# One pair of heads per TensorE round, one slot for V and two for K, in a cached decode block

## The chip, the cores and the metric

The kernel runs on one core of a Trainium2 chip. The metric is the device time of one execution in microseconds (us). The kernel before takes 1302.85 us, the median of three runs (1302.77 to 1302.91).

## The reference

The block decodes one token for two sequences. It has an attention part over a long cache and a small MLP, both with a layernorm ahead of them.

```python
def _A_ref(x, k_cache, v_cache, wq, wo):          # x: 2 x 1 x 512
    B, Sq, D = x.shape
    H, Dh = 32, 128                                # caches: 2 x 32 x 8192 x 128, f32
    q = (x @ wq).reshape(B, Sq, H, Dh).transpose(0, 2, 1, 3)
    scores = einsum("bhqd,bhkd->bhqk", q, k_cache) * (Dh ** -0.5)
    p = softmax(scores, axis=-1)
    o = einsum("bhqk,bhkd->bhqd", p, v_cache)
    return o.transpose(0, 2, 1, 3).reshape(B, Sq, H * Dh) @ wo

def _B_ref(x, w1, b1, w2, b2):
    y = layernorm(x)
    h = gelu(einsum("bsd,df->bsf", y, w1) + b1)    # F = 1792
    return einsum("bsf,fd->bsd", h, w2) + b2

h = x + _A_ref(layernorm(x), ...)
h2 = h + _B_ref(layernorm(h), ...)
```

Each cache holds 268 MB of float32, and each element of it is used once. The profile counts 561 MB of reads in all.

## The kernel before

**Units.** The work is cut into 32 units, `units[i] = (g, b)`: a pair of heads g (16 pairs) of one sequence b (2). The units 2g and 2g+1 belong to one pair; they are called the even and the odd unit of pair g below. The K of a unit is a tile of 128 partitions x 16384 f32 (8.39 MB; partitions 0 to 63 hold one head, 64 to 127 the other), and so is its V. I write K(i) and V(i) for them.

**What a unit does.** VectorE (DVE) multiplies K(i) by the broadcast query (`multiply`, L468), in two pieces of 80 and 48 rows in most units (`LONG`), and sums each row (`add_up`, L476); GpSimd (POOL) first adds the halves of the 80-row piece (`halve`, L472), so that DVE has half as much to sum there. `row_max` (L483) takes each partition's maximum and TensorE (PE) transposes it. After the odd unit, `all_max` (L488) takes the maxima of both units, `exps` makes the exponentials of both on ScalarE (ACT, L503), and `values` multiplies them on PE with V: 32 products (64 in the records, since a float32 product takes two passes) that fill four groups of 32 output partitions in turn. `values(2g)` stands right behind `exps(g)`; `values(2g+1)` stands in the next unit, behind its second `multiply`. `gather` copies the result to SBUF, `head_sum` adds its four parts on PE, and `head_out` (L543) scales with the softmax's denominator.

**Slots and the order of loads.** SBUF has room for three tiles of K or V: the three slots of `kv`, handed out in turn by `slot()`. Unit i asks for V(i-1) and then K(i+1), and one queue (SP) issues all of these loads in that order. A load can't be issued before the last reader of its slot is done, and SP takes its entries strictly in turn, so a load that waits holds up all behind it. Going round three slots, V(n) comes into the slot of K(n), and K(n+3) into the slot of V(n). `Waits` sets all semaphore waits from what each instruction reads and writes; a DMA counts on one of 12 semaphores (`LANES`), in turn.

**TensorE's loop.** `Rounds` records PE's instructions of units between `pe.round()` calls, and `end` (L200) requires each round to have the same addresses and to move its waits by the same steps; then it writes one round as a loop body. Before, a round holds `GH = 3` pairs, and there are five rounds; the PSUM and SBUF buffers come round to the same place after three pairs. 72 tiny products on zeros (`SPARE`), whose result nobody reads, stand ahead of the loop.

**The attention output on its way to `wo`.** `head_out` writes rows: 4 partitions (sequence x head), three pairs wide (`orow`). Every three pairs `turn` transposes them on PE and `turned` adds them to columns (`oall`). `stage` brings the queries of three pairs at a time to the partitions where `make_q` spreads them. Part of `wo` (`wog`) is fetched by an indirect DMA onto chosen partitions.

**The end.** In the last unit (31) `load_wo` fetches `wo` and V(30) follows; then come V(31) and the MLP's weights. `project_all` multiplies the heads with `wo`, and the MLP follows.

Of the kernel before, what the change touches and what calls it, by code (L numbers as in the profile page):

```python
# [12 lines left out]
P = 128  # L13
# [7 lines left out]
SPARE = 72  # L21
GP = 6
GH = 3
SR = 4
LW = 6
LEFT = (((3, 7), (9, 16), (20, 28), (44, 47), (54, 57), (67, 93), (101, 106), (110, 114), (118, 122)),)
# [12 lines left out]
class Waits:  # L39
    LANES = 12  # L40

    def __init__(self, nc):
        self.nc = nc
        self.sems, self.count, self.clock, self.after, self.mem, self.mask = ({} for _ in range(6))
        self.lane = {}
        self.off = False
        nc.push_inst_callback(self.seen)
# [63 lines left out]
    def skip(self, n):  # L111
        self.lane["hard"] += n
# [5 lines left out]
    def place(self, eng, op, areas):  # L118
        areas = [(x, w) for x, w in areas if x is not None]
        queue = (eng,)  # L120
        if "DMA" in op:
            kind = "soft" if eng == "Pool" else "hard"
            k = self.lane.get(kind, 0)
            self.lane[kind] = k + 1
            proc = (kind, k % self.LANES)
        else:
            proc = queue
# [33 lines left out]
    def close(self):  # L161
# [3 lines left out]
        last = ("hard", (self.lane["hard"] - 1) % self.LANES)  # L165
# [80 lines left out]
class Room:  # L246
# [3 lines left out]
    def tile(self, shape, dtype, name, tag=None, bufs=None, ahead=0):  # L250
# [6 lines left out]
        ring.append(ring.pop(ahead))  # L257
        v = ring[-1][:shape[0], :n]
# [6 lines left out]

    def turn(self, key, n):
        ring = self.held[key]
        ring[:] = ring[n:] + ring[:n]


def tile_decode_block(nc, waits, x, k, v, wq, wo, wog, w1, bias, w2, out):
# [10 lines left out]
    GL = NP - 1  # L282
    units = [(g, b) for g in range(NP) for b in range(B)]
# [11 lines left out]
    def slot():  # L295
        return kv.tile([P, ROW], F32, name="kv", tag="kv")
# [7 lines left out]
    wqt = slot()  # L304
# [3 lines left out]
    wgt = wts.tile([P, len(LEFT), SR, D], F32, name="wgt")  # L308
# [8 lines left out]
    orow = const.tile([4, GH, 2, DH], F32, name="orow")  # L317
    oall = const.tile([P, 2, 2 * GP, B], F32, name="oall")
    NQ = len(LEFT)
    og = const.tile([P, NQ * SR + LW - TH, B], F32, name="og")  # L320
    slots = [kept(x) for x in LEFT]
    first_slot = [sum(n for _, n in slots[:q]) for q in range(len(LEFT))]
    HG = H - LW
    NS = (HG - 4 * GP) * DH // SR
    assert sum(n for _, n in slots) == NS
# [3 lines left out]
    pms = {}  # L329
    for x in LEFT:  # L330
        if x not in pms:
            pms[x] = const.tile([P, P], F32, name=f"pm{len(pms)}")
            nc.gpsimd.memset(pms[x], 0.0)
            for p0, s0, n in kept(x)[0]:
                nc.gpsimd.tensor_copy(pms[x][:, p0:p0 + n], ident[:, s0:s0 + n])
    pm = [pms[x] for x in LEFT]
    FAR = 4096.0
    ioff = const.tile([P, len(LEFT)], F32, name="ioff")
    for q in range(len(LEFT)):
        nc.gpsimd.tensor_scalar(ioff[:, q:q + 1], pidx, first_slot[q] - FAR, None, op0=ALU.add)  # L340
# [9 lines left out]
    so2 = [psa.tile([P, 512], F32, name="so"), [psq.tile([P, 512], F32, name="qps") for _ in range(3)][2]]  # L350
# [5 lines left out]
    qs = const.tile([2 * B, GH, DH], F32, name="qs")  # L356
    wz = const.tile([P, B], BF16, name="wz")
    nc.gpsimd.memset(wz, 0.0)
# [9 lines left out]
    y2 = wgt[:B, 0, 0, :]  # L368
    nc.vector.tensor_scalar(y2, x2, mv[:, 0:1], rs, op0=ALU.subtract, op1=ALU.mult)

    ypt = psm.tile([P, DC, B], F32, name="sm")
# [4 lines left out]
    ipt = psm.tile([P, len(LEFT)], F32, name="sm")  # L376
    for q in range(len(LEFT)):
        pe.matmul(ipt[:, q:q + 1], pm[q], ioff[:, q:q + 1], start=True, stop=True)
# [8 lines left out]
    i4 = ident[:4, :4].rearrange("m (b s) -> m b s", s=2)  # L387
    hmask = const.tile([4, 2], F32, name="hmask")
    nc.vector.tensor_add(hmask, i4[:, 0, :], i4[:, 1, :])

    gidx = const.tile([P, len(LEFT)], mybir.dt.int32, name="gidx")
# [13 lines left out]
    QP, S, MX, MT, GM, LT, RL, SS, OP, OT, TP = ({} for _ in range(11))  # L405
# [5 lines left out]
    def stage(m):  # L411
        g = GH * min(m, NP // GH - 1) + 1
        n = next((n for n in range(1, GH) if (g + n) % NG == 0), 1)
        for at, n in ((0, n), (n, GH - n)):
            rows, cols = of_pair(g + at)
            src = q2[rows, cols.start:cols.start + n * DH]
            nc.vector.tensor_reduce(qs[:, at:at + n].rearrange("m k d -> m (k d)"), src[:, :, None], axis=AX.X, op=ALU.max)  # L417

    def make_q(g):
        QP[g] = psq.tile([P, B, DH], F32, name="qps")  # L420
        for b in range(B):
            rows, cols = of_pair(g)
            q = qs[:, (g - 1) % GH, :] if g else q2[rows, cols]
            pe.matmul(QP[g][:, b], pick[:2 * B, b, :], q, start=True, stop=True)

    make_q(0)
    stage(0)
    rowacc = psa.tile([B, D], F32, name="rowacc")
    for _ in range(SPARE):
        pe.matmul(rowacc[:, :B], wz, wz, start=True, stop=True)  # L430

    def load(src, i, parts):
        g, b = units[i]
        t = slot()
        rows = src[b, 2 * g:2 * g + 2].rearrange("h (p j) d -> (h p) (j d)", j=NS2)
        for s0, n in parts:
            nc.sync.dma_start(t[:, s0 * DH:(s0 + n) * DH], rows[:, s0 * DH:(s0 + n) * DH])
        return t

    def load_wo():  # L440
        t = slot()
        n = (2 * 2 * GP + LW) * D
        t = t[:, ROW - n:]
        nc.sync.dma_start(t, wo)
        for q in range(NQ):
            nc.gpsimd.indirect_dma_start(
                out=wgt[:, q].rearrange("p r n -> p (r n)"), out_offset=None,
                in_=wog,
                in_offset=bass.IndirectOffsetOnAxis(ap=gidx[:, q:q + 1], axis=0),
                bounds_check=NS - 1, oob_is_err=False)  # L450
        tv = t[:, :2 * 2 * GP * D].rearrange("p (j r n) -> p j r n", j=2, n=D)
        return tv, t[:, 2 * 2 * GP * D:].rearrange("p (r n) -> p r n", n=D)

# [24 lines left out]
    def row_max(i):  # L478
        g, b = units[i]
        if not b:  # L480
            MX[g] = work.tile([P, B], F32, name="mx", bufs=3)
            MT[g] = psm.tile([1, B, P], F32, name="sm")
# [3 lines left out]
    def all_max(g):  # L486
        gm = work.tile([1, B, 2], F32, name="gm", bufs=3)
        nc.vector.tensor_reduce(gm, MT.pop(g).rearrange("o b (s p) -> o b s p", s=2), axis=AX.X, op=ALU.max,  # L488
                                negate=True)
        GM[g] = psm.tile([P, B, 2], F32, name="sm")  # L490
# [15 lines left out]
    def total(g):  # L506
        RL[g] = psm.tile([4, 1] if g < GL else [P, 4], F32, name="sm")
        if g < GL:
            pe.matmul(RL[g], lt4, ones[:, 0:1], start=True, stop=True)
        else:  # L510
            pe.matmul(RL[g], ones, lt4, start=True, stop=True)

    def inverse(g):
        r = work.tile(list(RL[g].shape), F32, name="rl" if g < GL else "rlp")
# [17 lines left out]
    def head_sum(g):  # L532
        ss = SS.pop(g)
        OP[g] = psm.tile([4, DH] if g < GL else [P, 2 * B], F32, name="sm")
        for j in range(4):
            sj = ss[:, j * DH:(j + 1) * DH]
            a, w = (sel4[:, :, j], sj) if g < GL else (sj, sel4[:, :, j])
            pe.matmul(OP[g], a, w, start=(j == 0), stop=(j == 3))

    def head_out(g):  # L540
        op, rl = OP.pop(g), RL.pop(g)
        if g < GL:
            nc.vector.scalar_tensor_tensor(orow[:, g % GH], op[:, None, :].to_broadcast([4, 2, DH]), rl,  # L543
                                           hmask[:, :, None].to_broadcast([4, 2, DH]), op0=ALU.mult, op1=ALU.mult)
# [4 lines left out]
    def turn(j):  # L549
        rows = orow.rearrange("m k e d -> m (k e d)")  # L550
        if j < 4:
            TP[j] = psm.tile([HP, 2 * GP, 2 * B], F32, name="sm")
            rows = rows.rearrange("m (p r) -> m r p", r=2 * GP)
            for r in range(2 * GP):
                pe.transpose(TP[j][:, r, :], rows[:, r, :], ident[:4, :4])
            psm.turn("sm", 2)
            return
        TP[j] = psm.tile([P, NQ * SR + LW - TH, 2 * B], F32, name="sm")
        at, n = (HG - 4 * GP) * DH, LW - TH
        last = rows[:, at:at + n * DH].rearrange("m (p r) -> m r p", r=n)  # L560
        for r in range(n):
            pe.transpose(TP[j][:, NQ * SR + r, :], last[:, r, :], ident[:4, :4])
        rows = rows.rearrange("m (s r) -> m r s", r=SR)
        for q, (_, n) in enumerate(slots):
            s0 = first_slot[q]
            for r in range(SR):
                pe.transpose(TP[j][:n, q * SR + r, :], rows[:, r, s0:s0 + n], ident[:4, :4])

    def turned(j):
        if j < 4:  # L570
            tp = TP.pop(j)
            half = slice(HP * (j % 2), HP * (j % 2 + 1))
            nc.vector.tensor_reduce(oall[half, j // 2], tp.rearrange("p r (b s) -> p r b s", b=B), axis=AX.X, op=ALU.add)
            return
# [271 lines left out]
```

## Time and profile before

| what | value |
|---|---|
| median of three runs | 1302.85 us (1302.77 to 1302.91) |
| profiled execution, span from first to last instruction | 1301.3 us |
| mean granted TensorE clock | 0.638 |
| DMA | 561.17 MB, mean 431 GB/s |
| busy: DVE / PE / POOL / ACT | 976.5 / 384.8 / 366.5 / 49.3 us |

No own device time of the profiled execution is listed beside its span; the median of the runs lies 1.55 us above the span. A row of the timeline has the start and the duration in us, the engine, the line, the operation and its operands, and in brackets how long the engine had been idle and what ended that. A row of the chain of waits has start, duration and what was going on. "SPq" is SP's queue: the rows are the moments at which it issues a load.

### The profile page before, as it was taken

How to read it: one execution, taken by the hardware profiler on the slowest of the kernel's cores; microseconds unless marked ns; L12 is line 12 of the kernel's file. 1: busy time of each engine (PE TensorE's matmuls, PEld its weight loads, DVE VectorE, ACT ScalarE, POOL GpSimd, SP SyncE). 2: the span in 40 equal slices, each digit the busy share in tenths (PEclk: the TensorE clock that was granted, in tenths of full speed). 3: DMA queues.
4: the chain of work that ended last, by engine and by line, in shares of the span. 5: the costliest groups of instructions: out<-in, count | busy, mean ns of one | idle time of the engine just before them, and what ended most of it. 6: DMA issues, size and time to landing. Idle time of an engine off the chain costs nothing.

```text
span 1301.3 us, 6543 instructions
## 1 busy us (share of the span) xinstructions
PE 384.8 (30%) x2890; PEld 118.5 (9%) x2890; DVE 976.5 (75%) x291; ACT 49.3 (4%) x157; POOL 366.5 (28%) x67
## 2 busy tenths in 40 slices
PE   3105023230412314033330513323032331502359
PEld 0001000000100001010000101001010100100113
DVE  1988777779777779777779877778877778977752
ACT  0000000000000000000000000000000000000011
POOL 1433311333321333321233331233331133332320
PEclk9556566575666657566665666657566665756669
DMA  9999999999999999999999999999999999999998
GB/s 404 435 449 422 445 420 445 424 434 435 429 439 431 437 427 441 425 441 429 429 441 429 437 433 437 421 445 425 435 435 431 437 433 437 423 445 423 437 427 375
DMA packets 10824, 561.17 MB, mean 431 GB/s; under 512 B 1398, under 2 KB 1398, under 8 KB 1660
## 3 DMA queue, kind: packets, MB, share of 16 engines
q1 hardware_dynamic: 10664, 560.48, 99.7%
q0 software_dynamic: 144, 0.52, 0.1%
q8 instruction: 8, 0.13, 0.0%
q14 instruction: 4, 0.03, 0.0%
q10 hardware_dynamic: 4, 0.00, 0.0%
HBM read 561.53 MB, written 0.00 MB: 432 GB/s over the span
## 4 chain that ended last, share of the span: by engine, by line
DMA 45%; DVE 40%; PE 13%; ACT 1%; issue 1%; POOL 0%; SPq 0%; another core or an unknown queue 0%
DMA kv<-in_k_dram 40%; DVE kv L468 22%; DVE s L476 15%; PE so L239 10%; DMA kv<-in_w_dram 3%; DMA kv<-in_wq_dram 2%; PE sm L239 1%; ACT pt L503 1%; PE so L191 1%; DVE gm L488 0%; DVE orow L543 0%; DVE mx L483 0%; POOL kv L472 0%; DVE qs L417 0%; DVE nb L496 0%
## 5 line engine op out<-in xcount | busy, mean ns | idle before, releaser
L468 DVE TENSOR_TENSOR kv<-kv,qps 128x10240 f32<-128x10240 f32 (+1 forms) x68 | 555.5, 8171 | 238.5 <-DMA kv<-in_k_dram 238.3
L472 POOL TENSOR_TENSOR kv<-kv 128x5120 f32<-128x5120 f32 (+1 forms) x36 | 358.2, 9951 | 878.9 <-DVE kv L468 463.5
L476 DVE TENSOR_REDUCE s<-kv 128x48 f32<-128x6144 f32 (+1 forms) x68 | 380.6, 5636 | 1.2 <-POOL kv L472 0.3
L239 PE MATMUL so<-kv,pt 128*16 128x512 f32 x1920 | 275.8, 739 | 254.9 <-DMA kv<-in_v_dram 234.1
L239 PE MATMUL sm<-ident,mx 128*1 128x128 f32 x30 | 9.7, 325 | 583.2 <-DVE mx L483 583.2
L239 PEld LDWEIGHTS so<-kv,pt 128*16 128x16 f32 x1920 | 61.4, 113 | 444.4 <-DMA kv<-in_v_dram 235.6
L239 PEld LDWEIGHTS sm<-ident,mx 128*1 128x1 f32 x30 | 2.4, 79 | 589.4 <-DVE mx L483 586.7
L503 ACT ACTIVATE pt<-s,nb 64x128 f32<-64x128 f32 x64 | 25.5, 399 | 663.1 <-DVE nb L496 661.9
L530 ACT ACTIVATE ss<-so 128x512 f32<-128x512 f32 x16 | 9.6, 597 | 540.6 <-PE so L239 503.3
L239 PE MATMUL sm<-ss,sel 128*4 128x128 f32 x120 | 15.6, 272 | 12.5 <-ACT ss L530 12.5
L191 PE MATMUL qps<-kv,pt 128*16 128x512 f32 x128 | 17.0, 692 | 7.1 <-DMA kv<-in_v_dram 7.1
L403 DVE COPY q<-so 128x512 f32<-128x512 f32 x1 | 0.7, 692 | 19.3 <-PE so L191 19.3
L515 DVE RECIPROCAL rlp<-sm 128x4 f32<-128x4 f32 x1 | 0.2, 183 | 18.3 <-PE sm L191 18.3
L191 PE MATMUL qps<-kv 128*32 128x128 f32 (+2 forms) x178 | 13.2, 296 | 0.2 <-DMA kv<-in_w_dram 0.2
L488 DVE TENSOR_REDUCE gm<-sm 1x4 f32<-1x256 f32 x16 | 6.6, 413 | 7.3 <-PE sm L239 7.0
L239 PEld LDWEIGHTS sm<-ss,sel 128*4 128x4 f32 x120 | 9.3, 87 | 28.2 <-ACT ss L530 17.3
L191 PE MATMUL so<-kv,yT 128*4 128x512 f32 x64 | 8.5, 691 | 11.5 <-DMA kv<-in_wq_dram 11.5
L503 ACT ACTIVATION_READ_ACCUMULATOR pt<-s,nb 64x1 f32 x64 | 11.8, 185 | 0.0
L239 PE MATMUL qps<-qs,pick 4*128 4x128 f32 x60 | 11.1, 306 | 0.0
L239 PE MATMUL sm<-gm,srow 1*128 1x4 f32 x30 | 8.7, 359 | 7.6 <-DVE gm L488 7.6
L191 PE MATMUL so<-kv,oall 128*2 128x512 f32 x48 | 7.7, 805 | 8.7 <-DMA kv<-in_wo_dram 8.7
L496 DVE COPY nb<-sm 128x4 f32<-128x4 f32 x15 | 2.4, 162 | 10.1 <-PE sm L239 10.1
(121 smaller groups left out, 124.4 us busy)
## 6 DMA issues: line engine op xcount, KB each, us to landing
kv<-in_k_dram SPq DMA_DIRECT2D x2, 4096.0 KB, 36.4
kv<-in_wo_dram SPq DMA_DIRECT2D x1, 7680.0 KB, 28.2
kv<-in_v_dram SPq DMA_DIRECT2D x1, 6144.0 KB, 27.9
kv<-in_w_dram SPq DMA_DIRECT2D x1, 3584.0 KB, 35.9
kv<-in_v_dram SPq DMA_DIRECT2D x1, 2048.0 KB, 28.5
kv<-in_w_dram SPq DMA_DIRECT2D x1, 1792.0 KB, 39.8
kv<-in_w_dram SPq DMA_DIRECT2D x1, 1024.0 KB
kv<-in_w_dram SPq DMA_DIRECT2D x1, 512.0 KB, 42.6
```

The lines of the kernel that those rows point to most:

```text
L191: getattr(self.nc.tensor, what)(*aps, **how)
L239: ins = getattr(pe, what)(*aps, **how)
L403: nc.vector.tensor_copy(q2, so2[0])
L468: nc.vector.tensor_tensor(kc, kc, QP[g][:, b, None, :].to_broadcast([P, chunks(i)[c], DH]), op=ALU.mult)
L472: nc.gpsimd.tensor_tensor(kc[:, :, 0:HP], kc[:, :, 0:HP], kc[:, :, HP:DH], op=ALU.add)
L476: nc.vector.tensor_reduce(S[i][:, a:z], chunk(i, c, t)[:, :, 0:n], axis=AX.X, op=ALU.add)
L488: nc.vector.tensor_reduce(gm, MT.pop(g).rearrange("o b (s p) -> o b s p", s=2), axis=AX.X, op=ALU.max, negate=True)
L496: nc.vector.tensor_copy(nb, GM.pop(g))
L503: nc.scalar.activation(ptz[b][q, :, 4 * m:4 * m + 4], s[q], AF.Exp, bias=nb[q, b, e:e + 1], scale=SCALE, accum_out=lt4[q, m:m + 1])
L515: nc.vector.reciprocal(r, RL[g])
L530: nc.scalar.activation(SS[g], so2[g == GL], AF.Copy)
```

## The change

A round of PE's loop now holds one pair of heads, and there are 15 rounds. For every round to have the same addresses, the buffers get fixed places (`at=`): `slot(2)` for V(0) to V(30), `slot(0)` and `slot(1)` for the K of even and odd units, one PSUM bank each for the small products, one bank for the spread query. V(31) goes to slot 1. `stage` brings one pair's query each time, in the even unit. `head_sum` takes its operands the other way round for all pairs, as it did before for the last pair alone, so its result comes out as columns (128 partitions x 4), and `head_out` writes them to `oall` directly; `orow`, `turn` and `turned` go. One small product per half (`spread_out`) brings two heads to the partitions of the indirect load. The DMAs' semaphores are four in the loop and twelve in the last unit (`waits.late(12)`). The 72 unread products go. The rows of `wo` are laid out to match.

```diff
-SPARE = 72
-GP = 6
-GH = 3
...
-        ring.append(ring.pop(ahead))
-        v = ring[-1][:shape[0], :n]
+        if at is None:
+            ring.append(ring.pop(0))
+        v = ring[-1 if at is None else at][:shape[0], :n]
...
-    def slot():
-        return kv.tile([P, ROW], F32, name="kv", tag="kv")
+    def slot(at):
+        return kv.tile([P, ROW], F32, name="kv", tag="kv", at=at)
+
+    def bank(shape, at):
+        return psm.tile(shape, F32, name="sm", at=at)
...
-    def stage(m):
-        g = GH * min(m, NP // GH - 1) + 1
-        n = next((n for n in range(1, GH) if (g + n) % NG == 0), 1)
-        for at, n in ((0, n), (n, GH - n)):
-            rows, cols = of_pair(g + at)
-            src = q2[rows, cols.start:cols.start + n * DH]
-            nc.vector.tensor_reduce(qs[:, at:at + n].rearrange("m k d -> m (k d)"), src[:, :, None], axis=AX.X, op=ALU.max)
+    def stage(g):
+        rows, cols = of_pair(min(g, NP - 1))
+        nc.vector.tensor_reduce(qs, q2[rows, cols][:, :, None], axis=AX.X, op=ALU.max)
 
     def make_q(g):
-        QP[g] = psq.tile([P, B, DH], F32, name="qps")
+        QP[g] = psq.tile([P, B, DH], F32, name="qps", at=0)
...
-    for _ in range(SPARE):
-        pe.matmul(rowacc[:, :B], wz, wz, start=True, stop=True)
 
     def load(src, i, parts):
         g, b = units[i]
-        t = slot()
+        t = slot(i % 2 if src is k or i == NU - 1 else 2)
...
     def head_sum(g):
         ss = SS.pop(g)
-        OP[g] = psm.tile([4, DH] if g < GL else [P, 2 * B], F32, name="sm")
+        OP[g] = bank([P, 2 * B], 1)
         for j in range(4):
-            sj = ss[:, j * DH:(j + 1) * DH]
-            a, w = (sel4[:, :, j], sj) if g < GL else (sj, sel4[:, :, j])
-            pe.matmul(OP[g], a, w, start=(j == 0), stop=(j == 3))
+            pe.matmul(OP[g], ss[:, j * DH:(j + 1) * DH], sel4[:, :, j], start=(j == 0), stop=(j == 3))
 
     def head_out(g):
-        op, rl = OP.pop(g), RL.pop(g)
-        if g < GL:
-            nc.vector.scalar_tensor_tensor(orow[:, g % GH], op[:, None, :].to_broadcast([4, 2, DH]), rl,
-                                           hmask[:, :, None].to_broadcast([4, 2, DH]), op0=ALU.mult, op1=ALU.mult)
-            return
-        nc.vector.tensor_tensor(otz[:, :, 0:B], *(x.rearrange("p (b s) -> p s b", b=B) for x in (op, rl)),
+        to = oall[:, 2 * g:2 * g + 2, :] if g < GL else otz[:, :, 0:B]
+        nc.vector.tensor_tensor(to, *(x.rearrange("p (b s) -> p s b", b=B) for x in (OP.pop(g), RL.pop(g))),
                                 op=ALU.mult)
...
         if i == NU - 1:
-            wot, wlast = load_wo()
+            waits.late(12)
+            wot = load_wo()
...
                 if b == 0 and g >= 1:
                     inverse(g - 1)
+                    stage(g + 1)
                 if b == 1 and g >= 1:
                     head_out(g - 1)
                 elif b == 1:
-                    nc.vector.memset(orow, 0.0)
+                    nc.vector.memset(oall, 0.0)
...
-        if b == 0 and g % GH == 0 and g < GL:
+        if b == 0 and g < GL:
             pe.round()
         row_max(i)
```

The loads on SP's queue, the one place where the slots are seen. The rows show the tile with its slot (kv_0 to kv_2), the source, the size, and on which engine's semaphore the load waits. Before, from V(0) to V(2):

```order
L437 DMA kv_0<-in_v_dram 128x16384 [waits by_PE]
L437 DMA kv_1<-in_k_dram 128x16384 [waits by_DVE]
L437 DMA kv_2<-in_v_dram 128x16384 [waits by_DVE]
L437 DMA kv_0<-in_k_dram 128x16384 [waits by_PE]
L437 DMA kv_1<-in_v_dram 128x16384 [waits by_DVE]
```

And now, V(0) to K(4):

```order
L411 DMA kv_2<-in_v_dram 128x16384 [waits by_PE]
L411 DMA kv_0<-in_k_dram 128x16384 [waits by_DVE]
L411 DMA kv_2<-in_v_dram 128x16384 [waits by_PE]
L411 DMA kv_1<-in_k_dram 128x16384
L411 DMA kv_2<-in_v_dram 128x16384 [waits by_PE]
L411 DMA kv_0<-in_k_dram 128x16384 [waits by_DVE]
```

The order of the loads is the same; V(1), the third row of each piece, waited for DVE's last reader of K(1) and now waits for PE's last product with V(0). K(3) behind it needs no wait of its own any more.

On DVE, an odd unit and the start of the next even unit, before:

```order
L468 TENSOR_TENSOR kv_0<-kv_0,qps_1 128x10240
L543 SCALAR_TENSOR_TENSOR orow_0<-sm_2,rl_0,hmask_0 4x256
L468 TENSOR_TENSOR kv_0<-kv_0,qps_1 128x6144
L476 TENSOR_REDUCE s_0<-kv_0 128x48
L476 TENSOR_REDUCE s_0<-kv_0 128x80
L483 TENSOR_REDUCE mx_1<-s_0 128x1
L488 TENSOR_REDUCE gm_1<-sm_0 1x4
L496 COPY nb_1<-sm_1 128x4
L468 TENSOR_TENSOR kv_2<-kv_2,qps_2 128x10240
L515 RECIPROCAL rl_1<-sm_2 4x1
```

And now:

```order
L438 TENSOR_TENSOR kv_1<-kv_1,qps_0 128x10240
L507 TENSOR_TENSOR oall_0<-sm_1,rl_0 128x4
L438 TENSOR_TENSOR kv_1<-kv_1,qps_0 128x6144
L446 TENSOR_REDUCE s_0<-kv_1 128x48
L446 TENSOR_REDUCE s_0<-kv_1 128x80
L453 TENSOR_REDUCE mx_0<-s_0 128x1
L458 TENSOR_REDUCE gm_0<-sm_0 1x4
L466 COPY nb_1<-sm_1 128x4
L438 TENSOR_TENSOR kv_0<-kv_0,qps_0 128x10240
L482 RECIPROCAL rl_1<-sm_2 128x4
L394 TENSOR_REDUCE qs_0<-q2_0 4x128
```

In the odd unit the operation between the two multiplications has 4 elements per partition where it had 256; the one that stages a query now stands in each even unit.

More of the change, by code (lines that the diff above doesn't have):

```diff
@@ L248, in __init__, with tile @@
         self.nc, self.bufs, self.psum, self.held = nc, bufs, psum, {}
[L250 removed]
+    def tile(self, shape, dtype, name, tag=None, bufs=None, at=None):
         key = tag or name
@@ L349, in tile_decode_block @@
     nc.vector.memset(srow, SCALE)
-    so2 = [psa.tile([P, 512], F32, name="so"), [psq.tile([P, 512], F32, name="qps") for _ in range(3)][2]]
+    so2 = [psa.tile([P, 512], F32, name="so"), psq.tile([P, 512], F32, name="qps", at=2)]
     for t in so2:
@@ L374, in tile_decode_block @@
     nc.vector.tensor_copy(yT[:, :, B:2 * B], ypt)
-    ipt = psm.tile([P, len(LEFT)], F32, name="sm")
-    for q in range(len(LEFT)):
-        pe.matmul(ipt[:, q:q + 1], pm[q], ioff[:, q:q + 1], start=True, stop=True)
+    ipt = bank([P, 1], 1)
+    pe.matmul(ipt, pm[:, 0], ioff, start=True, stop=True)
     sel = const.tile([P, 16], F32, name="sel")
@@ L403, in tile_decode_block @@
     nc.vector.tensor_copy(q2, so2[0])
-    QP, S, MX, MT, GM, LT, RL, SS, OP, OT, TP = ({} for _ in range(11))
+    QP, S, MX, MT, GM, RL, SS, OP, TP = ({} for _ in range(9))
     def of_pair(g):
@@ L440, in load_wo @@
     def load_wo():
-        t = slot()
-        n = (2 * 2 * GP + LW) * D
-        t = t[:, ROW - n:]
+        t = slot(0)[:, ROW - (H - 2) * D:]
         nc.sync.dma_start(t, wo)
[L445 to L452, printed above, removed]
+        nc.gpsimd.indirect_dma_start(
+            out=wgt.rearrange("p r n -> p (r n)"), out_offset=None,
+            in_=wog,
+            in_offset=bass.IndirectOffsetOnAxis(ap=gidx, axis=0),
+            bounds_check=HP - 1, oob_is_err=False)
+        return t.rearrange("p (h n) -> p h n", n=D)
     def chunks(i):
@@ L506, in total @@
     def total(g):
-        RL[g] = psm.tile([4, 1] if g < GL else [P, 4], F32, name="sm")
-        if g < GL:
-            pe.matmul(RL[g], lt4, ones[:, 0:1], start=True, stop=True)
-        else:
-            pe.matmul(RL[g], ones, lt4, start=True, stop=True)
+        RL[g] = bank([P, 2 * B], 2)
+        pe.matmul(RL[g], ones, lt4, start=True, stop=True)
     def inverse(g):
-        r = work.tile(list(RL[g].shape), F32, name="rl" if g < GL else "rlp")
+        r = work.tile([P, 2 * B], F32, name="rl")
         nc.vector.reciprocal(r, RL[g])
@@ L586, in placed, with spread_out @@
+        nc.vector.tensor_tensor(to, *(x.rearrange("p (b s) -> p s b", b=B) for x in (OP.pop(g), RL.pop(g))),
+                                op=ALU.mult)
+    def spread_out():
+        TP[0] = bank([P, 2, 2 * B], 2)
+        for h in range(2):
+            pe.matmul(TP[0][:, h], pm[:, h], oall[:, GA:GA + 2, :].rearrange("p s b -> p (s b)"),
+                      start=True, stop=True)
     def placed():
-        nc.vector.tensor_copy(og[:, :NQ * SR], TP.pop(4))
-    def project_all(wot, wlast):
+        nc.vector.tensor_copy(og.rearrange("p r b -> p (r b)"), TP.pop(0).rearrange("p h m -> p (h m)"))
@@ L660, in tile_decode_block @@
             total(g)
-            if g % GH == 0 and g < GL:
-                turn(max(g // GH - 1, 0))
     vlast = load(v, NU - 1, [(0, 96), (96, 32)])
-    wt = slot()
+    wt = slot(0)
     br = wt[:, 2 * DC * F:2 * DC * F + FN + P]
@@ L679, in tile_decode_block @@
     nc.scalar.activation(junk[:, 0:1], lt4[:, 0:1], AF.Sqrt)
-    late = slot()
+    late = slot(2)
     at = [0]
@@ L801, in _laid_out @@
     d = wo.shape[1]
-    rows = 4 * GP * P
-    last = len(wo) - LW * P
-    own = last + (LW - TH) * P
+    heads = wo.reshape(-1, P, d)
+    at = len(heads) - LW - 2
+    plain = _np.concatenate([heads[:at], heads[at + 2:]])
+    some = heads[at:at + 2].reshape(2, 2, HP, d).transpose(2, 1, 0, 3)
     halves = (_NG, 32, 2, len(b1) // (64 * _NG))
```

149 lines of the change are left out of this document (45 added, 104 removed).

## The prediction

> **What bounds the kernel now.** I read the page's table of the span first: whatever sets the time must be busy in nearly all of the 40 slices.
>
> ```profile
> DVE  1988777779777779777779877778877778977752
> DMA  9999999999999999999999999999999999999998
> DMA packets 10824, 561.17 MB, mean 431 GB/s; under 512 B 1398, under 2 KB 1398, under 8 KB 1660
> q1 hardware_dynamic: 10664, 560.48, 99.7%
> ```
>
> The DMA engines are. SP's queue alone keeps all 16 busy for 99.7% of the span, and every other engine has gaps. Before, then, the time is the bytes over the rate, and work on an engine counts only where it makes a load start late. So the second view is the chain of waits, over one round of two units:
>
> ```profile
> 914.34 10.82 DVE kv L468
> 925.16 0.38 DVE orow L543
> ...
> 932.67 11.96 DVE s L476 x2
> ...
> 947.83 8.42 PE so L239 x62
> 956.25 0.15 PE sm L239
> 956.40 35.31 DMA kv<-in_k_dram
> 991.72 0.02 issue
> 991.74 10.82 DVE kv L468
> ```
>
> The chain closes on itself: an odd unit's K arrives, DVE works on it, softmax, PE's products with V, then the next odd unit's K is issued and arrives 35.31 us later. A load of that size takes far less, so most of the 35.31 us is waiting in the queue behind the V issued before it: that is the slack of this loop. How much there is shows in SP's timeline and DVE's, here for the round of pair 6 (K(13) is there at 527.23, K(14) at 565.93, K(15) at 604.64):
>
> ```profile
> 556.90 0.33 SPq L437 DMA_DIRECT2D kv<-in_v_dram  x1
> 569.68 0.33 SPq L437 DMA_DIRECT2D kv<-in_k_dram  x1
> 595.51 0.33 SPq L437 DMA_DIRECT2D kv<-in_v_dram  x1
> 595.88 0.44 SPq L437 DMA_DIRECT2D kv<-in_k_dram  x1
> ```
>
> ```profile
> 527.23 10.82 DVE L468 TENSOR_TENSOR kv<-kv,qps 128x10240 f32<-128x10240 f32 x1 [9.06 <-DMA kv<-in_k_dram]
> 537.97 0.47 DVE L543 SCALAR_TENSOR_TENSOR orow<-sm,rl,hmask 4x256 f32<-4x256 f32 x1
> 538.37 6.53 DVE L468 TENSOR_TENSOR kv<-kv,qps 128x6144 f32<-128x6144 f32 x1
> ...
> 565.93 10.82 DVE L468 TENSOR_TENSOR kv<-kv,qps 128x10240 f32<-128x10240 f32 x1 [7.02 <-DMA kv<-in_k_dram]
> 576.67 0.15 DVE L515 RECIPROCAL rl<-sm 4x1 f32<-4x1 f32 x1
> 576.75 6.52 DVE L468 TENSOR_TENSOR kv<-kv,qps 128x6144 f32<-128x6144 f32 x1
> ...
> 604.64 10.82 DVE L468 TENSOR_TENSOR kv<-kv,qps 128x10240 f32<-128x10240 f32 x1 [8.84 <-DMA kv<-in_k_dram]
> ```
>
> A round is 604.64 - 527.23 = 77.41 us, four loads, 19.35 us each. V(13) is issued at 556.90, when DVE has read the last of K(13); K(14) is still coming in until 565.93, so V(13) waits 9 us in a queue that never empties. K(15) is issued at 569.68, after PE's products with V(12), and still finds V(13) under way (PE gets V(13) at 585.31):
>
> ```profile
> 96.01 9.38 PE L239 MATMUL so<-kv,pt 128*16 128x512 f32 x64 [1.38 <-ACT pt L503]
> 560.10 9.44 PE L239 MATMUL so<-kv,pt 128*16 128x512 f32 x64 [1.39 <-ACT pt L503]
> 585.31 8.79 PE L239 MATMUL so<-kv,pt 128*16 128x512 f32 x64 [14.89 <-DMA kv<-in_v_dram]
> 637.50 9.99 PE L239 MATMUL so<-kv,pt 128*16 128x512 f32 x64 [1.39 <-ACT pt L503]
> 1180.05 8.38 PE L239 MATMUL so<-kv,pt 128*16 128x512 f32 x64 [1.38 <-ACT pt L503]
> ```
>
> **The change, part by part.** *V in one slot.* V(13) now goes where V(12) lies, so it can't be issued when DVE is done with K(13), but only when PE is done with V(12): at the moment at which K(15) was issued before. Queued behind it on SP is K(15), and nothing else is under way: V(12) and K(14) are the last loads ahead. I count from the moment T at which DVE starts on K(13):
>
> - T to the first product with V(12): 560.10 - 527.23 = 32.87 us. The odd unit's small DVE operation shrinks from 256 to 4 elements per partition. Before, the second multiplication started 0.32 us after the first one ended (538.37 against 527.23 + 10.82); in the even unit, with a 0.15 us RECIPROCAL at that place, it started with no delay (576.75 against 565.93 + 10.82). I take 0.31 us off: 32.56.
> - The products: of the 15 rows of this kind (pairs 0 to 14; the first and the last are shown) the shortest has 8.35, the longest 9.99 and the mean is 9.06 us. Sum 41.62.
> - From PE's last product to SP's issue: 569.68 - (560.10 + 9.44) = 0.14. V(13) is issued at T + 41.76.
> - K(14) has arrived by T + 38.70 (565.93 - 527.23). The queue has then been empty for 3.06 us, and V(13) must start it afresh.
>
> What a load takes on an empty queue is seen once, at the start, for `wq`, which has the same shape (128 x 16384) and is issued at 0.74; and, as the least, for the 4 KB output:
>
> ```profile
> kv<-in_wq_dram SPq DMA_DIRECT2D x1, 21.9
> ...
> out_dram<-kv SPq DMA_DIRECT2D x1, 4.0 KB, 1.4
> ```
>
> ```profile
> 22.69 8.49 PE L191 MATMUL so<-kv,yT 128*4 128x512 f32 x64 [11.51 <-DMA kv<-in_wq_dram]
> ```
>
> So V(13) takes 21.9 us from issue to landing, 2.55 more than behind another load. The bounds: 19.35 + 1.4 = 20.75 if only what a tiny load takes comes on top; 21.9 as the upper end. I take 21.9, a load of the same size and shape. K(15) follows behind it without a gap, 19.35, and the reader starts 0.05 after the landing (22.69 against 0.74 + 21.9). The next T: 41.76 + 21.9 + 19.35 + 0.05 = 83.06 us, against 77.41. That is **5.65 us more per round**, and there are 15 rounds from K(1) to K(31): 84.8 us. With the queue's bounds alone, 4.5 to 5.65 per round, it is 67 to 85.
>
> The Trainium skill ("DMA: Bandwidth & Descriptors", section "Anatomy of one DMA — SWDGE (gpsimd) path") gives a fixed cost of about 2.0 us for a DMA, whatever its size. By that, as an estimate, V(13) would take 21.35 us; the row of `wq` says 21.9, on SP's queue, and I go by the row.
>
> *The other half of the round.* V(14) now waits for the products with V(13). V(13) lands at T + 63.7, the products take up to 9.99, so V(14) is issued at T + 73.8, while K(15) is coming in until T + 83: hidden, with 9 us to spare. K(16) stands behind V(14) and needs K(14), which DVE has left at about T + 38.7 + 30 = T + 68.7: hidden.
>
> *One bank for the query.* `make_q` on PE now waits for the odd unit's second multiplication, T + 17.4. Behind it in PE's queue is the transposition of the odd unit's maximum at T + 29.7, and the query is needed at T + 38.7: nothing. The staged query, one small DVE operation per even unit, lies where DVE waits for K (7 to 9 us in the rows above): nothing; without that cover 0.3 us a round. The dropped `turn` and `turned` and the 72 unread products lay in waits of PE and DVE: no gain. PE's branch now comes after each pair, behind `head_sum` at about T + 75; the next thing needed from PE is at T + 83 + 17: nothing. Four DMA semaphores instead of twelve make a load wait for the one four earlier, two units ago: nothing.
>
> *The end.* The last odd unit starts here, and the rest hangs on it:
>
> ```profile
> 1224.22 4.42 DVE L468 TENSOR_TENSOR kv<-kv,qps 128x4096 f32<-128x4096 f32 x1 [9.34 <-DMA kv<-in_k_dram]
> ```
>
> `wo` and V(30) are queued before this moment (V(29) is used up by then, as V(13) was), V(31) goes to the slot of K(31) as before. The 77 us from there on are the same loads in the same order: no change.
>
> **Sum.** 1301.3 + 84.8 = 1386.1 us of span. The median of the runs lay 1.55 us above the span: 1387.7, say **1387**.
>
> **Rivals.** *A. The round locks to the clock of TensorE.* In one view over stretches of time (the column behind POOL's busy time is the granted clock) the clock changes at 565.30, 572.13, 589.20 and 599.44:
>
> ```profile
> 561.90:565.29 3.39, 3.39 (x24) 0.74 (x20) 0.00 (x0) 0.00 (x0) 0.00 (x0) 0.55 0.85 367
> 565.31:572.12 6.81, 5.10 (x54) 1.96 (x46) 6.19 (x1) 0.00 (x0) 0.00 (x0) 0.97 1.05 452
> 572.14:589.19 17.05, 3.88 (x20) 0.81 (x24) 16.99 (x5) 0.00 (x0) 11.05 (x1) 0.51 0.99 431
> 589.21:599.43 10.22, 6.75 (x61) 2.29 (x53) 6.56 (x3) 0.60 (x1) 0.00 (x0) 0.98 1.02 442
> ```
>
> The stretches between are 6.83, 17.07 and 10.24 us: 2, 5 and 3 times 3.413. So the clock steps on a grid of 3.413 us, and the products' time depends on where they start in it: from 560.10 the slow part lasts 5.20 us and the whole 9.44 = 6.84 + 5.20/2. Starting later by d, short of the next step, saves d/2. Now that these products are on the path, a round that starts late is shorter, and if 24 steps (81.92 us) can be had with products of 8.35 to 9.99 us, the round settles there. The rest of my round is 83.06 - 9.06 = 74.00; it would have to be below 81.92 - 8.35 = 73.57, so V(13)'s load at 21.47 or less instead of 21.9. That is inside my bounds. Price: (81.92 - 77.41) x 15 = 67.7, so 1370.5. Against it stands the one row for a load on an empty queue. The Trainium skill ("TensorE: Matmul & The Clock Gate", Part 1, "What's actually happening") has the grid as a free-running window of 3413 ns, half speed when idle, full after a busy window; the trace agrees with its 3.413 us. By the 2.0 us that the Trainium skill's "DMA: Bandwidth & Descriptors" gives, this rival would be the forecast.
>
> *B. More than the sum.* PE's loop fetches its code anew in each short round, or the restart costs more than `wq`'s did. For it: code was fetched in the first round; against it: none on that queue later, though the loop ran on.
>
> ```profile
> q8 instruction: 4, 0.07, 0.1%
> ```
>
> ```profile
> q14 instruction: 2, 0.02, 0.0%
> ```
>
> (The first row is from 60 to 300 us, the second from 300 to 1200, where q8 has none.) About 1 us more per round, for the 16 KB that one engine must move in between and the wait for it, gives 1402; from 1.3 us on, the round would settle at 25 steps, 85.33: +119, 1421.
>
> *C. Not slower.* This needs V(13) issued early enough to follow K(14) without a gap, at about T + 36.2 (38.70 less the 2.55 of a start), 5.6 us before my sum. The place where that could come from is PE's products: at full clock from the first, they take 6.84, 2.2 us less, and a round is still 80.8 (+51, 1354). Even a start at no cost on top leaves it at 78.3. So it takes a V load that doesn't wait for PE, which would leave the time at 1302 to 1303; the wait is there in the order of SP's loads. Nothing on the path of before gets shorter, so I see no way to faster.
>
> **How the numbers follow.** Forecast 0.57 (1380 to 1397: without the lock the mean of the products depends on how the starts fall on the grid, and 15 rounds of half a microsecond are 8 us); A 0.30; B 0.09; C 0.04, half of it for no change and 0.01 for faster. The range 1368 to 1398 holds the forecast and A. What a measurement of this kernel can tell from no change is about 0.2%, 2.6 us; slower by more has 0.97.
>
> **What would show it.** In the profile of the changed kernel: SP issues V (odd) and K 0.4 us apart, some 42 us after DVE's start on the odd K, no longer 12 to 13 us apart; DVE's starts on odd K are 83 us apart, from even to odd 44.3, from odd to even 38.7; the longest wait of DVE before an odd K grows from 9 to about 15 us; SP's queue falls from 99.7% to some 93% and the mean rate to 405 GB/s; in the chain, each round has the 10.82, the products and one DMA of some 41 us. Rounds of 81.92 us to the hundredth would be A. V issued while K is still landing, or rounds of 77.4, would prove me wrong.

## The result, and the profile after

The changed kernel takes 1391.16 us, the median of four runs (1389.17 to 1393.80); the kernel before took 1302.82 us beside it. The ratio is 1.068, with a 95% interval of 1.066 to 1.069: slower by 88 us. The profiled execution is that of the run of 1389.17 and has a span of 1387.3 us.

The page of the kernel after, its DMA rows:

```profile
DMA  9989989899898989989899898989989999898998
DMA packets 10821, 561.13 MB, mean 404 GB/s; under 512 B 1398, under 2 KB 1398, under 8 KB 1660
q1 hardware_dynamic: 10664, 560.48, 94.2%
...
q8 instruction: 5, 0.08, 0.0%
q14 instruction: 4, 0.03, 0.0%
```

The same bytes at 404 GB/s instead of 431, and SP's queue at 94.2% instead of 99.7%: the loads pause now. Where, the chain of waits shows, over one round of the kernel after (start, duration, what was going on):

```profile
643.46 10.82 DVE kv L438
654.28 0.07 DVE oall L507
...
660.85 11.96 DVE s L446 x2
...
676.02 9.95 PE so L235 x64
685.97 0.33 PE sm L235 x2
686.29 0.14 SPq L411
...
686.47 40.72 DMA kv<-in_k_dram
...
727.22 10.82 DVE kv L438
```

The chain has the same members as before. But the load that ends it takes 40.72 us where it took 35.31, since two whole loads, the odd V and the odd K, now start together. The timelines of SP, DVE and PE for this round of the kernel after:

```profile
686.10 0.33 SPq L411 DMA_DIRECT2D kv<-in_v_dram  x1
686.47 0.43 SPq L411 DMA_DIRECT2D kv<-in_k_dram  x1
717.43 0.33 SPq L411 DMA_DIRECT2D kv<-in_v_dram  x1
```

```profile
654.20 0.15 DVE L507 TENSOR_TENSOR oall<-sm,rl 128x4 f32<-128x4 f32 x1
654.27 6.54 DVE L438 TENSOR_TENSOR kv<-kv,qps 128x6144 f32<-128x6144 f32 x1
...
682.14 10.82 DVE L438 TENSOR_TENSOR kv<-kv,qps 128x10240 f32<-128x10240 f32 x1 [7.31 <-DMA kv<-in_k_dram]
...
727.22 10.82 DVE L438 TENSOR_TENSOR kv<-kv,qps 128x10240 f32<-128x10240 f32 x1 [14.97 <-DMA kv<-in_k_dram]
```

```profile
676.02 9.95 PE L235 MATMUL so<-kv,pt 128*16 128x512 f32 x64 [1.38 <-ACT pt L473]
707.92 9.36 PE L235 MATMUL so<-kv,pt 128*16 128x512 f32 x64 [21.64 <-DMA kv<-in_v_dram]
```

The even K has landed at 682.14, and the odd V is issued at 686.10, 0.4 us ahead of the odd K. In the view over stretches of time, whose last two columns are the DMA engines' share and the rate (a packet counts whole where it starts), the pause is plain to see:

```profile
682.00:687.20 5.20, 4.28 (x42) 1.17 (x34) 5.06 (x1) 0.00 (x0) 0.00 (x0) 1.00 0.23 76
...
688.50:700.00 11.50, 0.00 (x0) 0.00 (x0) 11.40 (x5) 0.00 (x0) 6.96 (x1) 0.51 0.96 416
```

The trace's records of single packets (64 KB each in these loads) show the pause itself: the 16 engines end their last packets of the even K between 681.22 and 681.75 us, and start the odd V between 687.08 and 688.12, 1.0 to 2.0 us after its issue at 686.10. Their first packets of it then take 2.41 to 3.37 us, where 2.42 is the rule. Over the first 14 rounds the engines stand still for 5.1 us a round on average, against 0.01 before, and their packets take 0.6 us longer: together the 5.7 us by which a round grew.

### The profile page after: what moved, and what is told of

It reads as the page before. It is cut to its first block, busy times and chain, and to the rows that moved or that the text cites. A ratio compares the mean times of both kernels' runs of the same rounds, so it can differ in the third digit from the quotient of the medians.

```text
span 1387.3 us, 6287 instructions
## 1 busy us (share of the span) xinstructions
PE 381.4 (27%) x2752; PEld 122.7 (9%) x2752; DVE 972.6 (70%) x287; ACT 49.3 (4%) x157; POOL 366.3 (26%) x66
## 3 DMA queue, kind: packets, MB, share of 16 engines
q1 hardware_dynamic: 10664, 560.48, 94.2%
## 4 chain that ended last, share of the span: by engine, by line
DMA 49%; DVE 36%; PE 12%; ACT 1%; POOL 1%; issue 1%; SPq 0%
DMA kv<-in_k_dram 44%; DVE kv L438 21%; DVE s L446 15%; PE so L235 10%; DMA kv<-in_w_dram 3%; DMA kv<-in_wq_dram 2%; PE sm L235 1%; ACT pt L473 1%; POOL kv L442 1%; PE so L187 1%; DVE gm L458 0%; DVE mx L453 0%; DVE nb L466 0%; SPq L411 0%; PE qps L187 0%
## 5 line engine op out<-in xcount | busy, mean ns | idle before, releaser
L235 PE MATMUL so<-kv,pt 128*16 128x512 f32 x1920 | 268.8, 723 | 347.8 <-DMA kv<-in_v_dram 327.1
L235 PE MATMUL qps<-qs,pick 4*128 4x128 f32 x60 | 18.3, 456 | 380.0 <-DVE kv L438 380.0
L235 PEld LDWEIGHTS qps<-qs,pick 4*128 4x128 f32 x60 | 13.8, 317 | 383.2 <-DVE kv L438 383.2
L235 PE MATMUL sm<-sel,ss 128*128 128x4 f32 x120 | 15.8, 255 | 12.1 <-ACT ss L497 12.1
L235 PEld LDWEIGHTS sm<-sel,ss 128*128 128x128 f32 x120 | 14.5, 191 | 25.9 <-ACT ss L497 25.9
L482 DVE RECIPROCAL rl<-sm 128x4 f32<-128x4 f32 x16 | 2.8, 176 | 16.4 <-PE sm L187 16.4
```

What stands on the lines that cost most here:

```text
L235: ins = getattr(pe, what)(*aps, **how)
L482: nc.vector.reciprocal(r, RL[g])
```

## Experiments: which part of the change

**The slots alone.** The kernel before, with three pairs per round, its rows of o and its padding, and only this edit:

```diff
-        t = slot()
+        t = slot(i % 2 if src is k or i == NU - 1 else 2)
```

(and fixed slots for `wq`, `wo` and the weights). Expected:

> The kernel before with the slots alone changed: V(0) to V(30) in slot 2, K in slots 0 and 1; rounds of three pairs, rows of o, padding as before. Theory (the odd V waits for PE's products with the even V, on an empty queue): rounds of about 83.4 us, since the odd unit keeps its 256-element operation (0.31 us) and in every third pair the staging (0.62 us): 1303 + 15 x 6 = about 1396 (1385 to 1402). Rival (the loop of one pair, with its branch or its code, costs the time): 1303, since the loop is as before.

Measured: 1398.96 us, ratio 1.074 (1.072 to 1.075), as the theory had it. Its SP timeline has the same pair of issues:

```profile
691.01 0.33 SPq L438 DMA_DIRECT2D kv<-in_v_dram  x1
691.38 0.43 SPq L438 DMA_DIRECT2D kv<-in_k_dram  x1
```

So the slots by themselves cost more than the whole change: 96 us. The 7.8 us between this run and the changed kernel fit what the rest of the change should be worth once DVE's odd unit is on the path: 0.31 us less in 15 rounds and a staging of 0.62 us gone from five odd units are 7.75 us, as an estimate. No run takes these two apart, and the runs of the changed kernel alone lie 4.6 us apart, so that the two numbers come this close is luck.

**All but the slots.** The changed kernel with the odd V back in the slot of the odd K, and two pairs per round, after which V's places repeat:

```diff
-        t = slot(i % 2 if src is k or i == NU - 1 else 2)
+        t = slot(0 if src is k and not b else (1 + g % 2 if b else 2 - g % 2))
...
-        if b == 0 and g < GL:
+        if b == 0 and g < GL and g % 2:
             pe.round()
```

> The changed kernel with the odd V back in the slot of the odd K (so it waits for DVE), the even V in the slot of the odd V before it (so it waits for PE), and two pairs per round, since V's place then repeats after two pairs; all else as changed. Theory: the odd V is issued 9 us before its turn, the even V has 9 us to spare too: 1302 to 1304, rounds of 77.4. Rival (something else in the change costs the time, such as the single banks, the staged query or four semaphores): 1391 stays.

Measured: 1303.35 us, ratio 1.0004 (0.9994 to 1.0014). SP and DVE in one of its rounds:

```profile
556.88 0.33 SPq L411 DMA_DIRECT2D kv<-in_v_dram  x1
568.66 0.33 SPq L411 DMA_DIRECT2D kv<-in_k_dram  x1
595.09 0.33 SPq L411 DMA_DIRECT2D kv<-in_v_dram  x1
```

```profile
527.52 10.82 DVE L438 TENSOR_TENSOR kv<-kv,qps 128x10240 f32<-128x10240 f32 x1 [8.59 <-DMA kv<-in_k_dram]
566.23 10.82 DVE L438 TENSOR_TENSOR kv<-kv,qps 128x10240 f32<-128x10240 f32 x1 [7.34 <-DMA kv<-in_k_dram]
604.93 10.82 DVE L438 TENSOR_TENSOR kv<-kv,qps 128x10240 f32<-128x10240 f32 x1 [8.60 <-DMA kv<-in_k_dram]
```

The odd V goes out at 556.88, 9 us before the even K lands, and a round is 77.41 us. The even V (595.09) does wait for PE here, as in the changed kernel, and still has 9.8 us to spare. The kernel before took 1302.77 us beside this run, so the single banks, the staged query, the columns of o, the four semaphores and a loop of two pairs together cost some 0.6 us at most; the loss comes with the odd V's wait for PE. (A loop of one pair is tested with the graded parts below.)

**The padding.** The kernel before with `SPARE = 0`:

> The kernel before without its 72 unread products ahead of the loop, all else as before. They lay in a wait of TensorE, and the loop's code was fetched in its first round alone: 1302.8 within 1 us. Rival (they set where the loop's code lies and their absence costs fetches in every round): 1310 and more.

Measured: 1302.75 us, ratio 1.0000 (0.9990 to 1.0009). The 72 products were neither a cost nor a help.

## Experiments: the time of the issue

**V in halves, V in quarters.** Each V is loaded in n parts of rows, and each part waits only for the products that read its place. (The runs that split a load also have more semaphores for their DMAs, 6 to 10 instead of four.)

```diff
-            VT[i - 1] = load(v, i - 1, full)
+            VT[i - 1] = load(v, i - 1, [(j * NS2 // n, NS2 // n) for j in range(n)])
```

> The changed kernel with each V loaded in two halves of rows, each half waiting only for the products that read its place. Theory: the first half can be issued after half of the products, some 5.0 to 6.6 us after their start instead of 9.1: the empty time of the queue falls from 5.6 to 2.0 to 3.1 us a round, rounds of 79.4 to 80.5: 1333 to 1350. Rival (the cost is not the time of the issue): 1391.

> As with the halves, in four quarters. Theory: the first quarter goes out about 3.5 us after the first product, 36.2 us after DVE's start on the odd K, before K(even) has landed at 38.7; the next quarters follow faster than a quarter's 4.84 us: rounds of 77.4 to 78, 1303 to 1310, with V in one slot and one pair per round. Rival (not the time of the issue): 1391.

Measured: 1335.05 us with halves (ratio 1.026, 1.024 to 1.027), as expected; 1327.13 us with quarters (ratio 1.019, 1.017 to 1.020), which is 17 us above the upper end. The rounds with quarters are 78.9 us on average (77.9 to 80.2), not 77.4 to 78. One of 78.1 us (SP, DVE):

```profile
731.51 6.01 SPq L411 DMA_DIRECT2D kv<-in_v_dram  x4
```

```profile
734.31 10.82 DVE L438 TENSOR_TENSOR kv<-kv,qps 128x10240 f32<-128x10240 f32 x1 [7.71 <-DMA kv<-in_k_dram]
```

The first quarter is issued 2.8 us before the even K has landed, as expected, and yet the engines paused. The single packets tell why. How many of the 16 DMA engines were moving data, as the mean over the quarter of a microsecond that starts there:

```
731.00 16.0   731.25 12.0   731.50  3.7   731.75  2.0   732.00  2.0
732.25  2.2   732.50 10.1   732.75 15.8   733.00 16.0
```

Fourteen engines are done with the even K between 731.30 and 731.67, the last two at 733.65 and 733.94, some 2.4 us later, and "landed" is what the last one says. I had counted from the landing. For these fourteen, a part that is issued at 731.51 comes too late: it starts on them between 732.47 and 732.79. The pause is not all of the 1.5 us that a round with quarters takes more than before. The engines stand still for 0.6 us a round on average (0 to 1.6). Another 0.4 us are the smaller packets: four of 16 KB take 4 x 611 = 2444 ns where one of 64 KB takes 2419, and each engine has 16 such rows of V in a round. The rest goes, as far as it can be told, with slow first packets behind a pause (0.85 to 1.43 us in this round instead of 0.61).

**Only the odd V, in graded parts.** If the late issue is what was left, a part that goes out some 2 us earlier must close the gap:

```diff
-            VT[i - 1] = load(v, i - 1, full)
+            VT[i - 1] = load(v, i - 1, full if i % 2 else [(0, 16), (16, 16), (32, 32), (64, 64)])
```

> The changed kernel with the odd V alone in four parts of 16, 16, 32 and 64 rows. The first goes out after 4 of the 32 products, 34.4 us after DVE's start on the odd K. In the run with quarters the first DMA engines were done with the even K 2.4 us before the last one, and the first quarter, at 36.3 us, came too late for these. If that is what was left there: no engine runs dry, rounds of 77.4 to 77.6, 1303 to 1307. If it was the size of the loads or their number: 1320 to 1330 as with quarters.

Measured: 1308.96 us, ratio 1.005 (1.003 to 1.007); 2 us above the expected range. SP and DVE in one of its rounds:

```profile
718.57 7.98 SPq L411 DMA_DIRECT2D kv<-in_v_dram  x4
```

```profile
683.99 10.82 DVE L438 TENSOR_TENSOR kv<-kv,qps 128x10240 f32<-128x10240 f32 x1 [8.83 <-DMA kv<-in_k_dram]
722.70 10.82 DVE L438 TENSOR_TENSOR kv<-kv,qps 128x10240 f32<-128x10240 f32 x1 [7.34 <-DMA kv<-in_k_dram]
761.64 10.82 DVE L438 TENSOR_TENSOR kv<-kv,qps 128x10240 f32<-128x10240 f32 x1 [8.84 <-DMA kv<-in_k_dram]
```

The first part goes out 4.1 us before the landing, at T + 34.58, and a round is 77.65 us, 0.24 more than before. The DMA engines no longer stand still (0.12 us at most in any round), so the pause is gone. The remainder lies in the stretch with the split V (38.94 against 38.71), and the smaller packets account for it: 8, 8, 16 and 32 KB take 312 + 312 + 613 + 1215 = 2452 ns instead of some 2419 for 64 KB, eight times per engine, 0.26 us. This run also leaves the even V whole; by the packets above, that is worth 0.2 of the 1.3 us between its rounds and those with quarters. One pair per round and V in one slot thus cost 6 us instead of 88, if the odd V's load is cut finely enough. No version beat the kernel before, whose loads never pause.

## Experiments: what is on the path

**TensorE's clock.** Unread products are put ahead of the products with the even V, so that the clock is up when they start:

```diff
                     make_q(g + 1)
+                    warm(30)
...
+            if g < GL: warm(1)
             all_max(g)
+            if g < GL: warm(5)
             exps(g)
```

> The changed kernel with unread products on TensorE ahead of the products with the even V (30 behind the spread query, 1 ahead of the maximum over both units, 5 behind it), so that the clock is already up when those start. Theory (these products lie on the path): they take 6.9 us instead of 9.1, rounds of 80.9 instead of 83.1: 1391 - 33 = 1358 (1352 to 1364). Rival (the path is DVE and the loads alone): 1391.

Measured: 1376.34 us, ratio 1.056 (1.054 to 1.058), less than half of the expected gain. PE's timeline in one of its rounds:

```profile
739.89 9.26 PE L235 MATMUL rowacc<-pick,ident 128*128 128x512 bf16 x30
751.04 0.27 PE L235 MATMUL sm<-ident,mx 128*1 128x128 f32 x1 [1.89 <-DVE mx L459]
...
752.14 2.31 PE L235 MATMUL rowacc<-pick,ident 128*128 128x512 bf16 x5
754.39 7.57 PE L235 MATMUL so<-kv,pt 128*16 128x512 f32 x64
```

The five products take 0.46 us each; the granted clock had fallen to 0.5 at 752.05, behind a pause of 1.89 us, and was up again at 755.46, one step of 3.41 us later. The rounds show more than the pause: from the second to the thirteenth they take 81.8 to 82.2 us, around the 24 steps (81.92) of rival A, so this run had settled on the clock's grid as well. A second version fills the pause with 36:

> As the warm run, with 36 unread products behind the spread query instead of 30. There the clock fell again in the pause of 1.9 us behind the 30: the 5 behind the maximum took 2.31 us, the products with V started 0.5 us late and took 7.5 us, so the issue of the odd V came only 1.0 us earlier, and the rounds were 1.1 us shorter. If that pause was the cause, the 36 close it, the issue comes 2.2 us earlier and the rounds are 80.9: 1358 (1354 to 1364). If the clock is not what the products' time hangs on, 1376 as before.

Measured: 1358.89 us, ratio 1.043 (1.041 to 1.046). The same rows, and SP's issue:

```profile
727.53 10.88 PE L235 MATMUL rowacc<-pick,ident 128*128 128x512 bf16 x36
738.68 0.27 PE L235 MATMUL sm<-ident,mx 128*1 128x128 f32 x1 [0.28 <-DVE mx L459]
...
739.77 1.25 PE L235 MATMUL rowacc<-pick,ident 128*128 128x512 bf16 x5
741.22 7.06 PE L235 MATMUL so<-kv,pt 128*16 128x512 f32 x64 [0.20 <-ACT pt L479]
```

```profile
748.40 0.33 SPq L417 DMA_DIRECT2D kv<-in_v_dram  x1
```

The five take 0.25 us each, the products with V 7.06 us, and rounds are 80.5 to 80.8 us in ten of the first eleven (in the next three the clock was late again, and they took 82.1). The odd V goes out 39.43 us after DVE's start in these ten rounds, 2.3 us earlier than the changed kernel's mean of 41.76, and the rounds are 2.4 us shorter than its 83.10. So microseconds of PE, which was busy for 30% of the span before, are paid in full here: they set when the odd V is issued.

**A later and an earlier odd unit.** One run puts a reduction of 1450 elements into DVE's odd unit, another lets DVE start 0.76 us earlier:

```diff
+                if b == 1 and g < GL:
+                    nc.vector.tensor_reduce(idle, wgt.rearrange("p r n -> p (r n)")[:, :1450], axis=AX.X, op=ALU.add)
```

```diff
-            KT[i + 1] = load(k, i + 1, full)
+            KT[i + 1] = load(k, i + 1, [(0, 123), (123, 5)])
```

> The changed kernel with one more DVE operation in each odd unit but the last (a reduction over 1450 elements, its result unread), about 1.6 us by the 1.19 us of one over 1024. Plain sum: rounds of 84.7, 1415. With the lock to the clock's grid: the rest of the round is 75.6, the products can fill it up to 25 steps = 85.33, and the rounds stay there to the hundredth: 1425, with runs that lie closer together than those of the changed kernel (4.6 us). Rival (DVE's odd unit is not on the path): 1391.

> The changed kernel with the last 5 of K's 128 rows per partition as a load of their own, so that DVE's first multiplication starts 0.76 us before the whole K has landed. Plain sum: rounds of 82.3, 1380. With the lock: the rest of the round is 73.3, below the 73.6 at which 24 steps fit: rounds of 81.92 to the hundredth, 1373. Rival (DVE's odd unit is not on the path): 1391.

Measured: 1422.05 us (ratio 1.092, 1.090 to 1.093; runs within 1.7 us) with the reduction, 1375.50 us (ratio 1.056, 1.054 to 1.058; runs within 1.6 us) with the earlier start. The rival, that DVE's odd unit is off the path, is out in both. DVE's starts on odd K, of the run with the reduction and then of the one with the earlier start:

```profile
572.75 10.82 DVE L439 TENSOR_TENSOR kv<-kv,qps 128x10240 f32<-128x10240 f32 x1 [16.51 <-DMA kv<-in_k_dram]
583.55 1.65 DVE L560 TENSOR_REDUCE idle<-wgt 128x1 f32<-128x1450 f32 x1
...
658.13 10.82 DVE L439 TENSOR_TENSOR kv<-kv,qps 128x10240 f32<-128x10240 f32 x1 [16.59 <-DMA kv<-in_k_dram]
```

```profile
639.13 10.82 DVE L438 TENSOR_TENSOR kv<-kv,qps 128x10240 f32<-128x10240 f32 x1 [12.91 <-DMA kv<-in_k_dram]
...
721.08 10.82 DVE L438 TENSOR_TENSOR kv<-kv,qps 128x10240 f32<-128x10240 f32 x1 [13.07 <-DMA kv<-in_k_dram]
...
802.95 10.82 DVE L438 TENSOR_TENSOR kv<-kv,qps 128x10240 f32<-128x10240 f32 x1 [13.00 <-DMA kv<-in_k_dram]
```

Rounds of 85.38, 81.95 and 81.87: near 25 and 24 steps of 3.413 us (85.33 and 81.92), not at the plain sums (84.7 and 82.3). They are not equal to the hundredth, as I had written; once settled, those with the earlier start scatter from 81.74 to 82.10, and those with the reduction slip out once (86.58) and come back from below. Both medians lie within 3 us of what the lock gives and 4.5 to 7 us from the plain sum. The trace's records of the granted clock show the lock directly: with the earlier start the clock rises 35.7 to 36.2 us after DVE's start on the odd K in each round from the fourth on, in the changed kernel anywhere from 35.3 to 38.4. So the lock is real where a whole number of steps fits, with a small scatter that I have not explained.

## Why the prediction was right

**The mechanism** was the one on record: the odd V can't be issued before PE is done with the even V, by then the queue has run dry, and a fresh start costs on top. The slots alone bring the whole loss, all but the slots brings next to none, and an earlier issue takes the loss away in steps (one part 1391, halves 1335, quarters 1327, graded 1309).

**The sum**, term by term. T to the first product: 32.56 us forecast, 676.02 - 643.46 = 32.56 measured. The products: 9.06 forecast, 9.08 the mean of the 15 rounds. To SP's issue: 0.14 and 0.13. The odd V on an empty queue, to its reader's start: 21.9 + 0.05 forecast, 707.92 - 686.10 = 21.82 in this round and 21.91 the median of 15. The odd K behind it: 19.35 and 727.22 - 707.92 = 19.30. The round: 83.06 forecast, and (1225.72 - 62.30) / 14 = 83.10 measured over the first 14. I had one row for a load on an empty queue and trusted it over the lower bound; it repeats within a tenth in 12 of the 15 rounds (the other three: 22.1 to 22.5). The Trainium skill ("DMA: Bandwidth & Descriptors", "Anatomy of one DMA — SWDGE (gpsimd) path") has a fixed cost of about 2.0 us. Here, on SP's queue, a start on an empty queue costs 21.91 - 0.05 - 19.35 = 2.5 us, and the half microsecond was what decided between the forecast and rival A.

**The last round** was summed like the others. It is 85.04 us long, two more than their mean:

```profile
1225.72 10.82 DVE L438 TENSOR_TENSOR kv<-kv,qps 128x10240 f32<-128x10240 f32 x1 [15.05 <-DMA kv<-in_k_dram]
...
1310.76 4.42 DVE L438 TENSOR_TENSOR kv<-kv,qps 128x4096 f32<-128x4096 f32 x1 [16.25 <-DMA kv<-in_k_dram]
```

```profile
1286.52 1.24 POOL L417 DMA_INDIRECT wgt<-in_wog_dram,gidx  x1 [0.20 <-issue]
```

The indirect load of `wog` is issued while V(29) and K(31) come in, and these two take 22.42 and 20.97 us, 0.5 and 1.6 more than the usual 21.91 and 19.35. The packets of `wog` run from 1290.9 to 1312.5 and take 1.28 us of the 16 engines' time, which is more than half of the two microseconds; no run leaves `wog` out, so the rest stays open. With it the span grew by 86.0 us, against 84.8. I put the end at no change: from the start on K(31) it is 76.5 us after and 77.1 before.

**The offset.** I added 1.55 us between span and median, as before. The profiled run's own time is 1.87 us above its span, and it is the fastest of four that lie 4.6 us apart, where those of the kernel before lie 0.14 apart. That the spread comes from where the products fall on the clock's grid is argued, not shown; that the two kernels of the DVE experiments, which settled near whole steps, spread by 1.6 and 1.7 us fits it. The median is 4.2 us above 1387: 1.2 are the span's, 0.3 the offset's, 2.0 the profiled run's distance from the median, and 0.7 I had rounded off.

**Rival A** did not come about: the rest of the round measured 83.10 - 9.08 = 74.02, above its 73.57. That it was a real neighbour is shown by the run in which DVE starts 0.76 us earlier. The Trainium skill ("TensorE: Matmul & The Clock Gate", Part 1, "What's actually happening") has a free-running window of 3413 ns; that rounds settle near 24 and 25 of them agrees with it. **B**: the code was not fetched in every round (q8 and q14, the queues of instruction code, have 9 packets in all on the page after), and with graded parts the same loop of one pair runs at 77.65. **C**: even with the clock up throughout, the round stays at 80.5 to 80.8, where I had worked out 80.8.

**Where I was wrong** was behind the prediction. With quarters I took the landing of the even K for the time at which the queue runs dry, when most engines were done 2.4 us earlier. In the prediction itself the same reading ("the queue has then been empty for 3.06 us") did no harm, because the sum goes from issue to landing and needs no time of running dry. Rival C's "about T + 36.2" for an issue without a gap rests on it too, and it was wrong: with quarters V goes out at about T + 36.3, and the engines still pause in most rounds; T + 34.6, with the graded parts, is early enough. In the first warm run I gave the clock no time to fall in a pause of 1.9 us.

## What to carry to other kernels

When a transfer-bound kernel gets fewer or fixed buffers, ask for each load whose last read it now waits for, and compare the time of that read with the time at which the load ahead of it ends. A slack of a few microseconds may not be enough (here, an issue 2.8 us before the landing still left a pause, and one 4.1 us before it left none), and without it every engine in that chain is on the path, however small its busy share. A load that comes late by a few microseconds can be cut so that its first part waits for the first readers only; count its deadline from the first DMA engine that runs dry, not from the landing.

## What was not expected of the hardware

The DMA engines need not finish a load together: 14 of 16 were done some 2.4 us before the last two in the round with quarters shown above, in a load of 19.35 us, while in the changed kernel's round all 16 ended within 0.53 us. And a loop whose next load waits for a burst of TensorE work can settle on the steps of that engine's clock: letting DVE start 0.76 us earlier shortened the round by about 1.1 (83.10 to some 82.0).
